# One temporary of a float64 conversion in PSUM, and two sums of block products written over their PSUM banks

## The chip, the cores and the metric

The kernel runs on one NeuronCore of a Trainium2 chip. The metric is the device time of one execution in microseconds (us), the median of several executions. The engines are named as in the profile: PE is TensorE (its weight loads stand apart as PEld), DVE is VectorE, ACT is ScalarE, POOL is GpSimd, SP is SyncE, whose queue issues nearly all DMAs.

## The reference

Three layers are computed one after the other. First a banded attention with a distance bias (2 batches, 8 heads, 768 positions, width 64). Then a mixture of experts over 1536 tokens, of which the reference is

```python
for e in range(E):                        # E = 4, D = 512, F = 1024
    h = np.maximum(x @ w1[e], 0.0)
    out += p[:, e:e + 1] * (h @ w2[e])
```

Then a last layer, whose weights `w_in`, `w_out` and `g_ln` arrive as float64:

```python
h = x @ w_in
sm = softmax(h); solu = h * sm
ln = (solu - mean) / sqrt(var + 1e-06) * g_ln
return (ln @ w_out).astype(np.float32)
```

## The kernel before, in words

There are two arms; the inputs choose the fast one (`fast_arm`), and only its instructions run. Names that begin with `f` (`fg`, `fhh`, `fhl`, `fr`, `fwS`) are its tiles.

**Precision.** Every float32 matrix is held as a high and a low part in float32r, and a product is three matmuls: high by high, high by low, low by high. A matmul has 128 rows, 128 columns of weights and 512 columns of tokens, and writes one PSUM bank (`fg`, six banks in turn).

**The mixture.** Each of the four experts is cut into two halves of the hidden width, so there are eight half experts, `he` 0 to 7; "period" below is one half expert. From `he` 1 on, one half expert is (`moe`, L490 ff.):

1. the tokens 1024 to 1535 in eight groups of 12 matmuls (`gemm_groups`): four groups "up" (`g1`, L450), each followed by a Relu on ACT that makes the high part `fhh` (L456) and a DVE instruction that makes the low part `fhl` (L457); then four groups "down" (`g2`, L469), each followed by a DVE product with the expert's weight (L479, into one of the two halves of `tmp2`) and a POOL addition to the accumulator in `scr` (L480). Down needs all four `fhl`;
2. the tokens 0 to 1023 upwards in 14 block products of 6 matmuls, 84 in all (`paired_groups`, L530), combined from sums of blocks. ACT copies three of the partial results to SBUF (`kept`, L535, in the buffer `kr`), DVE adds a kept one and a bank (L538), ACT takes the Relu (L517) and DVE makes the low part (L518);
3. the same tokens down: two times four groups of 12 matmuls (L469), each group with L479 on DVE and L480 on POOL.

So a half expert is 96 + 84 + 96 = 276 matmuls.

**Work done beside it.** After each group the function `tick` lays more work into the queues: weights of the next half expert are loaded (L265), their high part is made on ACT (L279) and their low part on POOL (L287); POOL forms sums of weight blocks (L328 to L331). Between them stands the conversion of the last layer's weights from float64 to two float32r parts, in 32 pieces of 256 numbers a partition (`from_f64`, `conv_steps`). A piece has the steps load (L354), nothing, `one` (L189 to L192), `both` (L196 to L198, and L360 for the second 16 pieces, which scales by `g_ln`), `parts` (L363, L364) and store (L367). Each counted tick does one step, and a new piece begins every third counted tick; the ticks after the second and third up group and most of those in the block products are not counted. So after nearly each down group DVE gets one of `one` (4 instructions), `both` (3 or 4) and `parts` (2). All DVE instructions stand in one queue that is worked through in order: whatever `tick` put ahead of an L479 or L457 is done first.

The conversion has two temporaries of 256 columns, `af` and `ff` (as integers `a` and `f`), both at the end of the SBUF buffer `kr` (columns 2048 to 2559). The raw piece `fr` holds 64-bit numbers, of which `high` and `low` are every second 32-bit word, and is overwritten by the two parts. Before the change all operands of all these instructions are in SBUF.

Besides the six banks of `fg`, two PSUM banks belong to the pool `ps3a`, opened before the mixture; its tile `h3` is first used by the last layer (`g3`, L664).

Of the kernel before, what the change touches and what calls it, by code (L numbers as in the profile page):

```python
# [8 lines left out]
F32 = mybir.dt.float32  # L9
# [6 lines left out]
ALU = mybir.AluOpType  # L16
# [34 lines left out]
def kernel(ctx, tc, ep, qk, vp, nn, pr, wall, w64, gl, out):  # L51
    nc = tc.nc
# [18 lines left out]
    gt = const.tile([128, 8], F32, name="gt")  # L71
# [12 lines left out]
    krf = kr.rearrange("p a b c -> p (a b c)")  # L84
# [29 lines left out]
    with tc.manual_schedule():  # L114
# [27 lines left out]
        def iota(cols, step, base, cm):  # L142
# [23 lines left out]
                                       op0=ALU.is_le, op1=ALU.mult)  # L166
        nc.vector.scalar_tensor_tensor(out=fi, in0=ng, scalar=float(NG_MAX), in1=flg[:, 1:2],
                                       op0=ALU.is_le, op1=ALU.mult)
# [5 lines left out]
        flag = nc.values_load(fi[:1, :1], min_val=0, max_val=1)  # L174


    def from_f64(raw):

        w = raw.bitcast(I32).rearrange("p (c w) -> p c w", w=2)
        low = raw.bitcast(U32).rearrange("p (c w) -> p c w", w=2)[:, :, 0]  # L180
        high = w[:, :, 1]
        af, ff = (krf[:, 2048 + 256 * j:2304 + 256 * j] for j in range(2))
        a, f = af.bitcast(I32), ff.bitcast(I32)
        halves = raw.bitcast(F32R).rearrange("p (w c) -> p w c", w=2)
        v = nc.vector

        def one():

            v.tensor_scalar(a, high, 3, 0x3FFFFFFF, op0=ALU.logical_shift_left, op1=ALU.bitwise_and)  # L189
            v.scalar_tensor_tensor(out=f, in0=high, scalar=-2 ** 30, in1=a, op0=ALU.bitwise_and, op1=ALU.bitwise_or)  # L190
            v.tensor_scalar(a, high, 0x7FFFFFFF, None, op0=ALU.bitwise_and)  # L191
            v.scalar_tensor_tensor(out=ff, in0=a, scalar=float(897 << 20), in1=ff, op0=ALU.is_ge, op1=ALU.mult)  # L192

        def two():

            v.tensor_scalar(a, f, -2 ** 23, None, op0=ALU.bitwise_and)  # L196
            v.scalar_tensor_tensor(out=af, in0=low, scalar=2.0 ** -52, in1=af, op0=ALU.mult, op1=ALU.mult)  # L197
            v.tensor_tensor(out=ff, in0=ff, in1=af, op=ALU.add)  # L198

        return one, two, ff, halves  # L200

    def stream(arm):

# [4 lines left out]
        st = St()  # L208
# [135 lines left out]
        def conv_steps():  # L344

            c = st.next_conv
            if c >= 32 or st.cvp is None:
                return None
            st.next_conv += 1
            raw = st.cvp.tile([128, 256], I64, tag="r64", name=f"{arm}r64", bufs=2)  # L350
            one, two, ff, halves = from_f64(raw)

            def load():
                nc.sync.dma_start(out=raw, in_=w64[c])  # L354

            def both():
                two()
                if c >= 16:
                    j = (c - 16) // 2
                    nc.vector.tensor_scalar(ff, ff, gt[:, j:j + 1], None, op0=ALU.mult)  # L360

            def parts():
                nc.vector.tensor_copy(out=halves[:, 0], in_=ff)  # L363
                nc.vector.tensor_tensor(out=halves[:, 1], in0=ff, in1=halves[:, 0].bitcast(F32), op=ALU.subtract)  # L364

            def store():
                nc.sync.dma_start(out=w_dram[c // 2, :, :, 256 * (c % 2):256 * (c % 2) + 256], in_=halves.bitcast(F32))  # L367
                st.stored += 1

            return [load, nothing, one, both, parts, store]  # L370
# [125 lines left out]
        def paired_groups(he, h1, h2):  # L496

            lo, hi = slice(0, HALF), slice(HALF, 2 * HALF)

            def raw_x(k0, cols):  # L500
                return [[x[:, k0 + j, cols] for j in range(2)] for x in (xh, xl)]

            right = {1: raw_x(0, lo), 2: raw_x(2, lo), 3: raw_x(2, hi), 4: raw_x(0, hi)}
            for i, f in ((5, 0), (6, 1), (7, 2)):
                right[i] = [[xt[:, f, b, j] for j in range(2)] for b in range(2)]
            banks, kept = {}, {}

            def left(q, i):
                n = 8 * he + 2 * q
                w, k0 = {1: (st.pieces[n], 0), 2: (st.pieces[n], 2), 4: (st.pieces[n + 1], 2), 6: (st.pieces["S", n], 0),  # L510
                         3: (st.pieces["S", n], 2), 7: (st.pieces["S", n + 1], 0), 5: (st.pieces["S", n + 1], 2)}[i]
                return w.rearrange("p w (k f) -> p w k f", k=4)[:, :, k0:k0 + 2]

            def hidden(src, dst, ft):
                th = st.hp.tile([128, HALF], F32R, tag="hh", name=f"{arm}hh")
                tl = st.hp.tile([128, HALF], F32R, tag="hl", name=f"{arm}hl")
                nc.scalar.activation(th, src, AF.Relu)  # L517
                nc.vector.scalar_tensor_tensor(out=tl, in0=src, scalar=0.0, in1=th.bitcast(F32),  # L518
                                               op0=ALU.max, op1=ALU.subtract)
                dst[0][ft], dst[1][ft] = th, tl  # L520

            def product(q, i):
                c = {1: "a", 6: "a", 7: "a", 4: "a", 2: "b", 5: "c", 3: "c"}[i]
                if i in (1, 2, 5):
                    banks[q, c] = st.psp.tile([128, 512], F32, tag="g", name=f"{arm}g")
                ps = banks[q, c]
                w, x = left(q, i), right[i]
                for j in range(2):
                    for m, (a, b) in enumerate(((0, 0), (0, 1), (1, 0))):
                        nc.tensor.matmul(ps, lhsT=w[:, a, j], rhs=x[b][j],  # L530
                                         start=(i in (1, 2, 5) and j == 0 and m == 0), stop=(j == 1 and m == 2),
                                         skip_group_check=(i not in (1, 2, 5)))
                if i in (1, 6, 7):
                    kept[q, i] = sc_b[(2 if i == 6 else 0) + q]
                    nc.scalar.copy(kept[q, i], ps)  # L535
                if i in (2, 7, 3):
                    t = kept[q, {2: 1, 7: 7, 3: 6}[i]]
                    nc.vector.tensor_tensor(out=t, in0=t, in1=banks[q, "b" if i == 2 else "c"], op=ALU.add)  # L538
                    hidden(t, *((h1, 2 * q) if i == 2 else (h2, 2 * q + 1) if i == 7 else (h2, 2 * q)))
                elif i == 4:  # L540
                    hidden(ps, h1, 2 * q + 1)

            for i in (1, 2, 6, 5, 7, 4, 3):
                for q in range(2):
                    product(q, i)
                yield i
            for j in range(4):
                st.free["R", j] = he + 1
            if he < NHE - 1:
                for q in (0, 2):  # L550
                    form_steps(8 * he + 8 + q, st.now)
            else:
                st.second += range(14)
# [71 lines left out]
    def rest_of_moe(st, arm, gen):  # L625
        with ExitStack() as es:
            st.hp = hp = es.enter_context(tc.tile_pool(name=f"{arm}h", bufs=8))
            st.wS = es.enter_context(tc.tile_pool(name=f"{arm}wS", bufs=1)).tile([128, 4, 2, 512], F32R, name=f"{arm}wS")
            st.cvp = es.enter_context(tc.tile_pool(name=f"{arm}cvp", bufs=2))
            st.ps3 = es.enter_context(tc.tile_pool(name=f"{arm}ps3a", bufs=1, space=PSUM))  # L630
            with tc.tile_pool(name=f"{arm}gps", bufs=6, space=PSUM) as psp:
                st.psp = psp
                for q in (0, 2):
                    st.form_steps(8 + q, st.now + 2)
                st.tick()
                for _ in gen:
                    pass
                st.drain()
            solu_layer(st, arm, hp)
# [107 lines left out]
    def fast_arm():  # L747
        st = stream("f")
        with ExitStack() as es:
# [328 lines left out]
            late.pop()()  # L1078
            tokens[0] = NT
        rest_of_moe(st, "f", gen)  # L1080


    def general_arm():
# [7 lines left out]
        with ExitStack() as es:  # L1091
# [11 lines left out]
            for i in range(NI):  # L1103
# [27 lines left out]
                for b in range(B):  # L1131
                    s = SLOTS.index((b, i))
                    for pr_ in range(4):
                        x = psX.tile([128, 128], F32, tag="x", name="gx")
                        for a in range(2):
# [34 lines left out]
                            for c in range(NI):  # L1170
# [5 lines left out]
                                                op=ALU.subtract)  # L1176
        st.x_forms()
        rest_of_moe(st, "g", moe(st, [(0, 512), (512, 512), (1024, 512)]))

    with tc.If(flag > 0) as cmp:  # L1180
# [77 lines left out]
```

## Time and profile before

| what | us |
|---|---|
| median of 3 runs (773.88 to 774.78) | 773.94 |
| the profiled execution's own time | 773.89 |
| its span in the profile | 772.0 |
| busy: PE, PEld | 746.5, 597.9 |
| busy: DVE, ACT, POOL | 565.2, 264.9, 337.7 |

Between the profiled time and the span lie 1.89 us outside the profile. A busy share is an average over stages. Of PE it overstates: matmuls are pipelined and each one's end is modelled, so that one of 128x512 is shown at 389 to 397 ns, while they start some 227 ns apart when nothing holds them up (48 in 10.89 us). The attention takes the span up to about 187 us, the mixture beside the conversion up to about 622 us, the last layer the rest.

### The profile page before, as it was taken

What the parts mean: (1) busy time and instruction counts of PE and PEld (TensorE: products, weight loads), DVE (VectorE), ACT (ScalarE), POOL (GpSimd) and SP (SyncE); (2) the same over time, 40 slices, a digit from 0 to 9 for tenths busy, and PEclk for the clock granted to TensorE, in tenths of its full rate; (3) what the DMA queues carried; (4) which work ended last, traced back from release to release, by engine and by line L of the source; (5) the groups of instructions that cost most, each with busy time, mean ns of one, the idle gap of its engine ahead of it and who ended that gap; (6) DMA issues with size and microseconds to landing.
All of it is one profiled execution on the core that took longest, in us unless ns stands there. A gap on an engine that the chain in (4) does not pass through costs nothing.

```text
span 772.0 us, 10562 instructions
## 1 busy us (share of the span) xinstructions
PE 746.5 (97%) x3710; PEld 597.9 (77%) x3710; DVE 565.2 (73%) x1052; ACT 264.9 (34%) x593; POOL 337.7 (44%) x310
## 2 busy tenths in 40 slices
PE   8889999999999999999999899989989999999997
PEld 5667766688888888888888688868868887888886
DVE  6777778522599879969979986996999646455541
ACT  5666655332313132142131213213132314233352
POOL 1000079365169439609817922970795272000001
PEclk9999999999999999999999899999998999999999
DMA  8443421112143233323423222332322650222221
GB/s 249 133 126 101 124 79 45 42 42 91 31 138 109 67 97 109 107 85 104 116 68 110 82 82 82 109 115 64 110 69 68 231 206 0 60 74 75 62 72 46
DMA packets 54015, 73.01 MB, mean 95 GB/s; under 512 B 7104, under 2 KB 31936, under 8 KB 53952
## 3 DMA queue, kind: packets, MB, share of 16 engines
q1 hardware_dynamic: 53392, 71.81, 29.9%
q8 instruction: 31, 0.51, 0.3%
q10 hardware_dynamic: 560, 0.43, 0.2%
q14 instruction: 32, 0.26, 0.1%
HBM read 56.46 MB, written 11.56 MB: 88 GB/s over the span
## 4 chain that ended last, share of the span: by engine, by line
PE 62%; DVE 21%; issue 9%; ACT 4%; POOL 3%; DMA 0%; DVEq 0%; POOLq 0%; ACTq 0%
PE fg L469 19%; PE fg L530 13%; PE fo L725 9%; PE fh L664 7%; PE fg L450 5%; DVE tmp L479 4%; PE sps L816 3%; PE x L885 3%; DVE kr L190 3%; DVE kr L197 2%; PE pt L863 2%; DVE kr L191 2%; POOL scr L480 2%; DVE fhl L518 1%; POOL xl L483 1%
## 5 line engine op out<-in xcount | busy, mean ns | idle before, releaser
L469 PE MATMUL fg<-fhh,wV 128*128 128x512 f32 (+1 forms) x800 | 255.1, 391 | 0.0
L480 POOL TENSOR_TENSOR scr<-scr,tmp 128x512 f32<-128x512 f32 x84 | 112.2, 1338 | 174.9 <-DVE tmp L479 174.9
L469 PEld LDWEIGHTS fg<-fhh,wV 128*128 128x128 f32 x800 | 152.5, 191 | 35.2 <-issue 6.3
L469 PE MATMUL fg<-fhl,wV 128*128 128x512 f32 (+1 forms) x400 | 155.7, 389 | 10.3 <-DVE fhl L457 10.0
L450 PE MATMUL fg<-xh,wR 128*128 128x512 f32 (+1 forms) x320 | 102.7, 387 | 1.4 <-DVE xl L897 1.4
L469 PEld LDWEIGHTS fg<-fhl,wV 128*128 128x128 f32 x400 | 76.5, 191 | 28.4 <-DVE fhl L457 14.1
L450 PEld LDWEIGHTS fg<-xh,wR 128*128 128x128 f32 x320 | 59.9, 188 | 17.1 <-issue 4.3
L479 DVE TENSOR_TENSOR tmp<-fg,pb 128x512 f32<-128x512 f32 x84 | 57.3, 682 | 13.2 <-PE fg L469 8.4
L450 PE MATMUL fg<-xl,wR 128*128 128x512 f32 (+1 forms) x160 | 60.6, 379 | 0.0
L841 ACT ACTIVATE p<-p,mn 128x256 f32<-128x256 f32 (+1 forms) x96 | 46.3, 484 | 41.1 <-DVE mn L835 38.6
L530 PE MATMUL fg<-xt,fwS 128*128 128x512 f32 x252 | 58.3, 389 | 0.0
L535 ACT COPY kr<-fg 128x512 f32<-128x512 f32 x42 | 23.8, 581 | 97.3 <-PE fg L530 95.7
L530 PE MATMUL fg<-xh,wR 128*128 128x512 f32 x168 | 55.1, 394 | 0.0
L530 PEld LDWEIGHTS fg<-xt,fwS 128*128 128x128 f32 x252 | 47.3, 188 | 9.8
L279 ACT CAST fwS<-kr 128x512 fp32r<-128x512 f32 x28 | 16.0, 619 | 111.0 <-POOL kr L331 111.0
L714 POOL TENSOR_SCALAR fva<-fva 128x1 f32<-128x1 f32 x12 | 3.8, 313 | 109.3 <-ACT scr L713 109.3
L518 DVE SCALAR_TENSOR_TENSOR fhl<-kr,fhh 128x512 fp32r<-128x512 f32 x42 | 29.1, 693 | 29.4 <-ACT fhh L517 29.4
L287 POOL TENSOR_TENSOR wR<-fraw,wR 128x512 fp32r<-128x512 f32 x28 | 39.9, 1433 | 18.2 <-ACT wR L279 18.2
L517 ACT ACTIVATE fhh<-kr 128x512 fp32r<-128x512 f32 x42 | 26.6, 632 | 59.3 <-DVE kr L538 59.3
L725 PE MATMUL fo<-xt,fth 128*128 128x512 f32 (+1 forms) x156 | 45.3, 375 | 0.0
L190 DVE SCALAR_TENSOR_TENSOR kr<-fr,kr 128x256 int32<-128x256 int32 x32 | 43.3, 1353 | 1.1
L538 DVE TENSOR_TENSOR kr<-kr,fg 128x512 f32<-128x512 f32 x42 | 28.6, 681 | 20.3 <-ACT kr L535 18.8
(156 smaller groups left out, 1434.2 us busy)
## 6 DMA issues: line engine op xcount, KB each, us to landing
fraw<-in_wall_dram SPq DMA_DIRECT2D x61, 256.0 KB, 2.7
fr<-in_w_dram SPq DMA_DIRECT2D x32, 256.0 KB, 2.7
w_dram<-fr SPq DMA_DIRECT2D x32, 256.0 KB, 2.4
kr<-in_wall_dram SPq DMA_DIRECT2D x28, 256.0 KB, 2.6
v<-in_vp_dram SPq DMA_DIRECT2D x10, 512.0 KB, 3.4
xt<-w_dram SPq DMA_DIRECT2D x6, 512.0 KB, 10.2
kr<-in_qk_dram SPq DMA_DIRECT2D x22, 128.0 KB, 4.0
out_dram<-scr SPq DMA_DIRECT2D x11, 256.0 KB, 2.2
```

What stands on the lines that cost most here:

```text
L190: v.scalar_tensor_tensor(out=f, in0=high, scalar=-2 ** 30, in1=a, op0=ALU.bitwise_and, op1=ALU.bitwise_or)
L287: e.tensor_tensor(out=w[:, 1], in0=t, in1=w[:, 0].bitcast(F32), op=ALU.subtract)
L450: nc.tensor.matmul(ps[:, :n], lhsT=w[:, a, k], rhs=b[:, k, cols], start=(k == 0 and i == 0), stop=(k == 3 and i == 2))
L469: nc.tensor.matmul(ps[:, :n], lhsT=w[:, a, k], rhs=b[k], start=(k == 0 and i == 0), stop=(k == 3 and i == 2))
L479: nc.vector.tensor_tensor(out=t, in0=ps[:, :n], in1=pb[:, cols], op=ALU.mult)
L480: nc.gpsimd.tensor_tensor(out=a, in0=a, in1=t, op=ALU.add)
L518: nc.vector.scalar_tensor_tensor(out=tl, in0=src, scalar=0.0, in1=th.bitcast(F32), op0=ALU.max, op1=ALU.subtract)
L530: nc.tensor.matmul(ps, lhsT=w[:, a, j], rhs=x[b][j], start=(i in (1, 2, 5) and j == 0 and m == 0), stop=(j == 1 and m == 2), skip_group_ch ...
L538: nc.vector.tensor_tensor(out=t, in0=t, in1=banks[q, "b" if i == 2 else "c"], op=ALU.add)
L664: nc.tensor.matmul(ps[:, hf], lhsT=a[:, k, cs], rhs=w[:, b], start=(k == 0 and i == 0), stop=(k == 3 and i == 2))
L725: nc.tensor.matmul(ps, lhsT=a[:, fc % 4], rhs=wo[fc][:, b, c0:c0 + n], start=(fc == 0 and i == 0), stop=(fc == 7 and i == 2))
L841: nc.scalar.activation(p[:, a, :nw], p[:, a, :nw], AF.Exp, bias=mn[:, a:a + 1], scale=-1.0, accum_out=su[:, a:a + 1])
```

## The change

Two things change; no instruction is added, removed or moved, on any engine. (On DVE the last addition of the conversion, L198, keeps its place; its output is another tile.)

- The temporary `af` moves to PSUM: the tile `cvs` of two banks with the tag `h3` of the pool `ps3a`; piece c uses the first 256 columns of bank c % 2. `ff` stays in SBUF, now at columns 2048 to 2303. The last step's result is left in `af`: by the addition itself in the first 16 pieces, by the scaling in the other 16. So every two-input instruction of the conversion has one input in SBUF and one in PSUM, and every one-input instruction either writes or reads PSUM.
- Of the three sums in the block products (products 2, 7 and 3) those of 2 and 3 are written over the PSUM bank that was one of their inputs, instead of over the kept SBUF buffer. The Relu (L517) and the low part (L518) then read PSUM. Product 7's sum stays in SBUF, since its bank goes on accumulating.

```diff
-    def from_f64(raw):
+    def from_f64(raw, af):
...
-        af, ff = (krf[:, 2048 + 256 * j:2304 + 256 * j] for j in range(2))
+        ff = krf[:, 2048:2304]
...
-        def two():
+        def two(scale):
 
             v.tensor_scalar(a, f, -2 ** 23, None, op0=ALU.bitwise_and)
             v.scalar_tensor_tensor(out=af, in0=low, scalar=2.0 ** -52, in1=af, op0=ALU.mult, op1=ALU.mult)
-            v.tensor_tensor(out=ff, in0=ff, in1=af, op=ALU.add)
+            if scale is None:
+                v.tensor_tensor(out=af, in0=ff, in1=af, op=ALU.add)
+            else:
+                v.tensor_tensor(out=ff, in0=ff, in1=af, op=ALU.add)
+                v.tensor_scalar(af, ff, scale, None, op0=ALU.mult)
+
+        def parts():
+            v.tensor_copy(out=halves[:, 0], in_=af)
+            v.tensor_tensor(out=halves[:, 1], in0=af, in1=halves[:, 0].bitcast(F32), op=ALU.subtract)
...
-            one, two, ff, halves = from_f64(raw)
+            one, two, parts, halves = from_f64(raw, st.cvs[:, c % 2, 0:256])
...
-                    t = kept[q, {2: 1, 7: 7, 3: 6}[i]]
-                    nc.vector.tensor_tensor(out=t, in0=t, in1=banks[q, "b" if i == 2 else "c"], op=ALU.add)
+                    s, u = kept[q, {2: 1, 7: 7, 3: 6}[i]], banks[q, "b" if i == 2 else "c"]
+                    t = s if i == 7 else u
+                    nc.vector.tensor_tensor(out=t, in0=s, in1=u, op=ALU.add)
...
+            st.cvs = st.ps3.tile([128, 2, 512], F32, tag="h3", name=f"{arm}cvs")
```

## Rows read from the trace of the kernel before

**Rows 1.** The page: busy time, share of the span, instructions of two engines.
```profile
PE   746.5 (97%) x3710; PEld 597.9 (77%) x3710; DVE 565.2 (73%) x1052; ACT 264.9 (34%) x593; POOL 337.7 (44%) x310
```

**Rows 2.** Waits of PE: line, releaser, us in total, times, longest us.
```profile
PE fg L469 <- DVE fhl L457: 10.0, 7, 1.7
```

**Rows 3.** Chain of waits in time, 190 to 622: start us, us, what.
```profile
248.08 10.28 PE fg L469 x44
...
311.28 10.26 PE fg L469 x44
...
374.44 10.28 PE fg L469 x44
384.72 19.21 PE fg L530 x84
403.94 10.89 PE fg L469 x48
...
441.05 12.76 PE fg L469 x44
...
510.11 10.31 PE fg L469 x44
...
576.76 13.13 PE fg L469 x44
```

**Rows 4.** Windows: stretch, its length; busy PE, PEld, DVE, ACT, POOL; clock, DMA.
```profile
406.83:437.62 30.79, 29.97 (x133) 24.48 (x131) 30.10 (x37) 7.40 (x14) 26.98 (x24) 1.00 0.32 98
441.10:447.90 6.80, 6.80 (x19) 5.39 (x20) 6.59 (x11) 0.00 (x0) 4.23 (x4) 0.61 0.47 154
509.40:516.20 6.80, 6.09 (x27) 5.01 (x28) 6.66 (x11) 0.00 (x0) 5.04 (x4) 1.00 0.48 142
```

**Rows 5.** Timeline of DVE, 403 to 443: start us, us, engine, line, instruction.
```profile
406.83 0.68 DVE L479 TENSOR_TENSOR tmp<-fg,pb 128x512 f32<-128x512 f32 x1
...
433.59 1.40 DVE L197 SCALAR_TENSOR_TENSOR kr<-fr,kr 128x256 f32<-128x256 uint32 x1
435.02 1.40 DVE L198 TENSOR_TENSOR kr<-kr 128x256 f32<-128x256 f32 x1
...
437.62 0.68 DVE L457 SCALAR_TENSOR_TENSOR fhl<-fg,fhh 128x512 fp32r<-128x512 f32 x1
...
440.32 1.87 DVE L457 SCALAR_TENSOR_TENSOR fhl<-fg,fhh 128x512 fp32r<-128x512 f32 x3
```

**Rows 6.** Timeline of POOL, same stretch.
```profile
433.37 1.34 POOL L480 TENSOR_TENSOR scr<-scr,tmp 128x512 f32<-128x512 f32 x1
434.66 1.47 POOL L287 TENSOR_TENSOR wV<-fraw,wV 128x512 fp32r<-128x512 f32 x1
```

**Rows 7.** DVE by line: count, shortest/median/longest ns, first and last start, shape.
```profile
L190 DVE SCALAR_TENSOR_TENSOR kr<-fr,kr x32: 853/1401/1420, 193.5 to 612.9; 128x256 int32<-128x256 int32 x32
L191 DVE TENSOR_SCALAR kr<-fr x32: 293/296/1278, 194.9 to 614.4; 128x256 int32<-128x256 int32 x32
L198 DVE TENSOR_TENSOR kr<-kr x32: 424/1392/1411, 198.0 to 617.9; 128x256 f32<-128x256 f32 x32
L479 DVE TENSOR_TENSOR tmp<-fg,pb x84: 676/679/693, 187.1 to 631.6; 128x512 f32<-128x512 f32 x84
```

**Rows 8.** DVE L518 by line, its first input in SBUF (kr) or in PSUM (fg).
```profile
L518 DVE SCALAR_TENSOR_TENSOR fhl<-kr,fhh x42: 691/693/695, 200.8 to 611.4; 128x512 fp32r<-128x512 f32 x42
L518 DVE SCALAR_TENSOR_TENSOR fhl<-fg,fhh x14: 681/682/684, 212.1 to 607.4; 128x512 fp32r<-128x512 f32 x14
```

**Rows 9.** Timeline of SP, same stretch: a store and the next load.
```profile
417.22 0.53 SPq L367 DMA_DIRECT2D w_dram<-fr  x1
...
419.70 0.33 SPq L354 DMA_DIRECT2D fr<-in_w_dram  x1
```

**Rows 10.** Waits of DVE line L479, by line: releaser, us in total, times.
```profile
  POOL scr L480: 4.7, 2
```

**Rows 11.** DMA issues, 403 to 443: KB each, median us to landing.
```profile
fr<-in_w_dram SPq DMA_DIRECT2D x4, 256.0 KB, 2.6
```

More of the change, by code (lines that the diff above doesn't have):

```diff
@@ L192, in one @@
             v.scalar_tensor_tensor(out=ff, in0=a, scalar=float(897 << 20), in1=ff, op0=ALU.is_ge, op1=ALU.mult)
-        def two():
+        def two(scale):
             v.tensor_scalar(a, f, -2 ** 23, None, op0=ALU.bitwise_and)
             v.scalar_tensor_tensor(out=af, in0=low, scalar=2.0 ** -52, in1=af, op0=ALU.mult, op1=ALU.mult)
-            v.tensor_tensor(out=ff, in0=ff, in1=af, op=ALU.add)
-        return one, two, ff, halves
+            if scale is None:
[6 more added lines that the diff above has]
+            v.tensor_tensor(out=halves[:, 1], in0=af, in1=halves[:, 0].bitcast(F32), op=ALU.subtract)
+        return one, two, parts, halves
     def stream(arm):
@@ L356, in both @@
             def both():
[L357 to L364, printed above, removed]
+                two(gt[:, (c - 16) // 2:(c - 16) // 2 + 1] if c >= 16 else None)
             def store():
```

## The prediction

> **What bounds the kernel now.** I read the page's busy times first: PE is busy for 97% of the span, DVE for 73% [rows 1]. PE's own waits come next: in the whole span it lost time worth naming to one partner alone, the low part `fhl` (L457, DVE), 7 times, 10.0 us [rows 2]. That sum is too small, since an issue gap counts as idle only from a matmul's modelled end, so I take the loss from the chain of waits. It gives the pace without a stall: 84 matmuls of the block products in 19.21 us, 48 of the down groups in 10.89 us [rows 3]. A half expert is 84 + 4 x 48 matmuls, hence 19.21 + 4 x 10.89 = 62.77 us. The same chain marks six points at which PE went on behind a late `fhl`: 248.08, 311.28, 374.44, 441.05, 510.11 and 576.76 us. The five distances are 63.20, 63.16, 66.61, 69.06 and 66.65 us, which is 0.43, 0.39, 3.84, 6.29 and 3.88 us over the pace, 14.83 us together.
>
> Why is `fhl` late? Take the period before 441.05. DVE's first down product starts at 406.83 and the first L457 at 437.62 [rows 5]. PE ended the up group that this L457 belongs to at about 403.94 + 9 x 2.72 = 428.4 (2.72 us = a quarter of 10.89), so DVE is 9 us behind. In those 30.79 us DVE was busy for 30.10 [rows 4]: 8 products of 0.68 us (5.4 us) and 28 instructions of the conversion, which took 30.79 - 5.4 = 25.4 us, **0.905 us each** with their gaps.
>
> Why does one take that long? The shortest L198, with two SBUF inputs, took 0.424 us, the median 1.392; L190 and L191 scatter likewise, L191 from 0.293 to 1.278 [rows 7]. Beside it on the clock: L197 starts at 433.59 and ends at 434.99, L198 at 435.02 and ends at 436.42 [rows 5]; POOL's instructions end at 434.71 and 436.13 [rows 6]. Each DVE instruction ends 0.28 us behind the POOL instruction that was running when it began: it was held until POOL let go. L479 has the same kind of operation on twice the columns, but one input in PSUM, and all 84 took 0.676 to 0.693 us [rows 7], POOL running or not. So the wait belongs to instructions whose operands are all in SBUF.
>
> **The change, part by part.**
>
> *Conversion.* No instruction is added, so the sum is 28 instructions of a new length. After the change none has all operands in SBUF. For two inputs, one of them in PSUM, I halve L479's columns: by L198's shortest (0.424 for 256 columns) and SBUF against PSUM at 512 (0.693 against 0.682, [rows 8]) it is 0.41 to 0.42. For one input, out of or into PSUM: 0.42 too. It loses the fast form of 0.29 [rows 7], which I take to be lost with PSUM. No row shows DVE writing PSUM. Bounds: 0.29 below (today's fast form), 1.42 above (L190's longest, held by POOL) [rows 7]; I take 0.42, nearest to L198's shortest and L479. With a gap of 0.03 (434.99 to 435.02) 28 of them make 12.6 us, with the products 18.0, in place of 30.8. From the first product to the end of the first up group DVE has 428.4 - 406.8 = 21.6 us, so L457 starts when ACT has its Relu. Within one group's 2.72 us the longest lot is four instructions and a product, 4 x 0.45 + 0.68 = 2.5 us: nothing piles up.
>
> The point from which it decides: PE ends the fourth up group at 403.94 + 12 x 2.72 = 436.6 and needs the first `fhl` there, so L457 (0.68) may start at 435.9 at the latest; (435.9 - 406.83 - 5.4) / 28 = **0.84 us** an instruction. Twice my estimate still hides it.
>
> [...]
>
> *What goes.* The stalls, and with them a loss of clock. [...] So the terms are:
> - the five distances above: 14.83 us, of which 12.76 - 10.31 = 2.45 is clock;
> - the stall that ends at 248.08, alike in place to the next two: 0.43 us;
> - the slow stretch behind 576.76: 13.13 - 10.28 = 2.85 us.
>
> Together **18.1 us**, 12.8 of stalls and 5.3 of clock.
>
> *Covers.* A faster DVE asks earlier for the raw pieces. Today a store goes out at 417.22 and the load into its buffer at 419.70 [rows 9], landing 2.6 us later [rows 11]. Afterwards `parts` of the first piece follows the third product: PE's group ends at 403.94 + 3 x 2.72 = 412.1, plus 0.68 + 2 x 0.45 gives 413.7; store and load end at 413.7 + 2.5 + 2.6 = 418.8. The piece is wanted behind the seventh product, at 423.0 + 0.68 = 423.7. Cover: 4.9 us; without it DVE, and all in its queue, would wait for the rest.
>
> *Two sums over their banks.* 28 of the 42 low parts read PSUM: 0.011 us less each, 0.3 us of DVE in all [rows 8], in stretches where PE waits for nothing (the 84 matmuls hold their pace). The banks are held longer, until a Relu and a low part (0.69 us, [rows 8]) have read them; the next groups on them come after others, and need those same low parts anyway. I put it at zero; if a bank were wanted at once, it would cost some two times 0.69 us a half expert.
>
> *The rest.* Attention and last layer keep their instructions. Sum: 773.89 (the profiled execution, 0.05 below the median) - 18.1 = **755.8 us**.
>
> **The rivals.**
>
> *POOL becomes the late one.* It was busy 26.98 of the 30.79 us [rows 4], and L479 has already waited for its additions twice, 4.7 us [rows 10], since `tmp2` has two halves only. Against it: POOL's time there seems to include waits for DVE that go too (1.47 us beside 1.34 for the same size, [rows 6]), and L457 has 435.9 - 428.4 = 7.5 us, less one Relu, to spare. If it leaves half of the three long stalls (1.9 us each) and one slow stretch (2.6), it is 755.8 + 5.7 + 2.6 = 764.1.
>
> *The clock falls all the same.* Two slow stretches, not tied to stalls: 755.8 + 5.3 = 761.1. For: behind one of three equal stalls it did not fall, so stalls alone don't set it. Against: behind the three short stalls the 44 matmuls kept their 10.26 to 10.28 us [rows 3].
>
> *PE's lateness only changes hands*, or the SBUF operand that remains is held by POOL as before: no change, 773.9.
>
> *Slower.* The wait for POOL stays in the conversion whatever the operands, and the one-input instructions lose their fast form: of the 28, 14 (L189, L191, L196, L360, L363) go from 0.29 to 0.42, 1.8 us; in the first three periods, without L360, 11, 1.4 us. DVE is already over the point of 0.84, so all of it turns into stall: 3 x 1.8 + 3 x 1.4 = 9.6, **783.5 us**. [...] Against the mechanism stand the 84 L479, none above 0.693 us, though they read SBUF and write it beside POOL.
>
> **How the numbers follow.** Forecast 0.77 (with the spread of the single terms 754.3 to 757.5), POOL 0.08, clock 0.07, no change 0.04, slower 0.04. The range from 754.0 to 761.5 takes in the forecast and the clock, and leaves out 0.16. Faster by over 0.2% (1.5 us, about what a measurement of this kernel can tell from no change): 0.92; within it 0.04; slower 0.04.
>
> **What would show it.** Right: the conversion's lines all near 0.42 us and none near 1.4, DVE's busy time down by more than 100 us (304 instructions at 0.45 us less would be 138, too much since the early pieces wait less), no wait of PE for L457, six periods of about 62.8 us, granted clock 1.00 in all of them. POOL's additions should shorten too. Wrong: instructions that write PSUM at 0.84 us or more; PE's wait for L457 still there with L479 waiting for POOL; a clock of 0.6 without a stall before it; the time made up again behind 622 us.

## The result, and the profile after

The changed kernel took **755.51 us** (median of 4 runs, 755.48 to 755.99) against 773.91 us beside it (772.49 to 774.78): a ratio of 0.9765, 95% interval 0.9749 to 0.9782. Forecast were 755.8 us and a range of 754.0 to 761.5. The profiled execution took 755.48 us with a span of 753.7, 18.3 below the span before.

The page: busy time of the engines, then the shares of the chain that ended last, by engine.

```profile
PE 738.7 (98%) x3710; PEld 594.7 (79%) x3710; DVE 447.2 (59%) x1052; ACT 265.0 (35%) x593; POOL 321.5 (43%) x310
...
PE 93%; ACT 2%; DVE 2%; DMA 0%; POOL 0%; issue 0%; ACTq 0%
```

DVE lost 118 us of busy time [rows 1] and POOL 16, though neither has an instruction less; the chain now runs through PE almost alone (PE had 62% of it before and DVE 21%). (The lines of code have moved: L450 is now L451, L456 L457, L457 L458, L469 L470, L479 L480, L480 L481, L482 L483, L483 L484, L517 L518, L518 L519, L530 L531, L535 L536, L538 L540, and L363 and L364 are L205 and L206.)

The waits of PE, longest first; the last of these lines is the only one that the mixture beside the conversion has left, the first two lie in the attention.

```profile
PE wp L135 <- DVE eps L137: 1.4, 1, 1.4
PE fg L451 <- DVE xl L900: 1.4, 1, 1.4
...
PE fg L531 <- ACT kr L536: 1.0, 1, 1.0
```

The line of [rows 2], the wait for the low part, is gone. The chain of waits in order of time (start us, us, what) answers to [rows 3]:

```profile
246.92 10.88 PE fg L470 x48
...
309.65 10.88 PE fg L470 x48
...
372.38 10.88 PE fg L470 x48
383.25 19.23 PE fg L531 x84
402.48 21.76 PE fg L470 x96
424.24 10.88 PE fg L451 x48
435.12 10.88 PE fg L470 x48
...
497.85 10.88 PE fg L470 x48
...
560.58 10.88 PE fg L470 x48
571.46 2.73 PE fg L531 x12
```

Every half expert now takes 62.73 us, five times running, at PE's pace without a stall. From 185 to 640 us the chain has 44 pieces; before it had 518, many of them through DVE.

The DVE instructions by line (count, shortest/median/longest ns), to be held against [rows 7]; `fcvs` is the temporary in PSUM:

```profile
L189 DVE TENSOR_SCALAR fcvs<-fr x32: 415/417/419, 193.1 to 595.4; 128x256 int32<-128x256 int32 x32
L190 DVE SCALAR_TENSOR_TENSOR kr<-fr,fcvs x32: 420/420/422, 193.5 to 595.9; 128x256 int32<-128x256 int32 x32
L191 DVE TENSOR_SCALAR fcvs<-fr x32: 427/427/428, 194.0 to 596.3; 128x256 int32<-128x256 int32 x32
L192 DVE SCALAR_TENSOR_TENSOR kr<-fcvs,kr x32: 423/424/424, 194.4 to 596.8; 128x256 f32<-128x256 int32 x32
L202 DVE TENSOR_SCALAR fcvs<-kr,gt x16: 486/489/491, 410.0 to 599.5; 128x256 f32<-128x256 f32 x16
L205 DVE CAST fr<-fcvs x32: 411/414/416, 203.2 to 600.9; 128x256 fp32r<-128x256 f32 x32
L206 DVE TENSOR_TENSOR fr<-fcvs,fr x32: 423/424/425, 203.6 to 601.3; 128x256 fp32r<-128x256 f32 x32
```

Where a line had spread from 0.3 or 0.4 to 1.4 us, no two executions of it now differ by more than 5 ns. POOL's additions (L481) keep their median, 1.293 us against 1.296 before, but the long ones are gone: the longest takes 1.327 us, where it had taken 1.484, and the mean falls from 1.338 to 1.294. DVE's waits in the mixture name no load of a raw piece, so the cover that the prediction worked out held.

The same stretch as in [rows 4] and [rows 5], from the first down product to the first low part, in the windows (columns as in [rows 4]) and in DVE's timeline:

```profile
405.40:427.60 22.20, 22.20 (x100) 18.39 (x99) 16.73 (x36) 5.20 (x10) 19.63 (x19) 1.00 0.32 102
```

```profile
405.31 0.69 DVE L480 TENSOR_TENSOR tmp<-fg,pb 128x512 f32<-128x512 f32 x1
...
425.18 0.69 DVE L480 TENSOR_TENSOR tmp<-fg,pb 128x512 f32<-128x512 f32 x1 [1.15 <-POOL scr L481]
...
427.69 0.69 DVE L458 SCALAR_TENSOR_TENSOR fhl<-fg,fhh 128x512 fp32r<-128x512 f32 x1
428.30 0.41 DVE L205 CAST fr<-fcvs 128x256 fp32r<-128x256 f32 x1
428.75 0.42 DVE L206 TENSOR_TENSOR fr<-fcvs,fr 128x256 fp32r<-128x256 f32 x1
430.41 0.69 DVE L458 SCALAR_TENSOR_TENSOR fhl<-fg,fhh 128x512 fp32r<-128x512 f32 x1 [1.24 <-ACT fhh L457]
```

From first product to first low part it is 22.4 us now, it was 30.8; and DVE is idle for a quarter of the window. From the second low part on DVE waits for ACT's Relu, that is, for PE.

One wait is new. Here are POOL's and ACT's timelines of the last half expert, where POOL also makes the low part `xl` of the finished accumulator (L484) from the high part that ACT copies (L483):

```profile
574.17 1.29 POOL L484 TENSOR_TENSOR xl<-scr,xh 128x512 fp32r<-128x512 f32 x1 [0.73 <-PE fg L531]
575.42 1.29 POOL L481 TENSOR_TENSOR scr<-scr,tmp 128x512 f32<-128x512 f32 x1
```

```profile
576.75 0.62 ACT L483 CAST xh<-scr 128x512 fp32r<-128x512 f32 x1 [2.65 <-POOL scr L481]
577.27 1.07 ACT L536 COPY kr<-fg 128x512 f32<-128x512 f32 x2
```

PE needs ACT's copy of a block product (L536) at about 576.7 us. It stands in ACT's queue behind the copy of `xh`, that one waits for POOL's fourth addition, and that one stands in POOL's queue behind a low part that waited for ACT's previous copy (573.48 to 574.10; this row puts the wait down to PE, those of the other three groups to ACT's `xh`). One group of this exchange takes 3.27 us (573.48 to 576.75 for L483), a down group on PE 2.72. The next matmul starts 1.40 us behind the last instead of 0.23, by the starts in the trace, and the one after it 0.34: a loss of 1.17 + 0.11 us.

### The profile page after: what moved, and what is told of

Read it like the earlier page. It is cut to its first block, busy times and chain, and to the rows that moved or that the text cites. A ratio compares the mean times of both kernels' runs of the same rounds, so it can differ in the third digit from the quotient of the medians.

```text
span 753.7 us, 10598 instructions
## 1 busy us (share of the span) xinstructions
PE 738.7 (98%) x3710; PEld 594.7 (79%) x3710; DVE 447.2 (59%) x1052; ACT 265.0 (35%) x593; POOL 321.5 (43%) x310
## 4 chain that ended last, share of the span: by engine, by line
PE 93%; ACT 2%; DVE 2%; DMA 0%; POOL 0%; issue 0%; ACTq 0%
PE fg L470 35%; PE fg L531 18%; PE fg L451 14%; PE fo L728 9%; PE fh L667 9%; PE sps L819 3%; PE x L888 3%; PE pt L866 2%; ACT p L844 1%; DVE p L838 1%; ACT pts L868 0%; PE fpt L708 0%; DVE xl L900 0%; PE wp L959 0%; PE g L907 0%; DMA kr<-in_qk_dram 0%
## 5 line engine op out<-in xcount | busy, mean ns | idle before, releaser
L470 PE MATMUL fg<-fhh,wV 128*128 128x512 f32 (+1 forms) x800 | 251.3, 385 | 0.0
L481 POOL TENSOR_TENSOR scr<-scr,tmp 128x512 f32<-128x512 f32 x84 | 108.4, 1294 | 165.0 <-DVE tmp L480 165.0
L470 PEld LDWEIGHTS fg<-fhh,wV 128*128 128x128 f32 x800 | 149.9, 188 | 34.5 <-issue 6.3
L470 PE MATMUL fg<-fhl,wV 128*128 128x512 f32 (+1 forms) x400 | 152.4, 381 | 0.0
L451 PE MATMUL fg<-xh,wR 128*128 128x512 f32 (+1 forms) x320 | 102.7, 387 | 1.4 <-DVE xl L900 1.4
L480 DVE TENSOR_TENSOR tmp<-fg,pb 128x512 f32<-128x512 f32 x84 | 57.9, 690 | 58.6 <-PE fg L470 51.0
L470 PEld LDWEIGHTS fg<-fhl,wV 128*128 128x128 f32 x400 | 75.2, 188 | 13.8
L451 PEld LDWEIGHTS fg<-xh,wR 128*128 128x128 f32 x320 | 59.9, 188 | 17.1 <-issue 4.3
L458 DVE SCALAR_TENSOR_TENSOR fhl<-fg,fhh 128x512 fp32r<-128x512 f32 (+1 forms) x40 | 26.6, 664 | 57.8 <-ACT fhh L457 57.7
L451 PE MATMUL fg<-xl,wR 128*128 128x512 f32 (+1 forms) x160 | 60.6, 379 | 0.0
L531 PE MATMUL fg<-xt,fwS 128*128 128x512 f32 x252 | 58.4, 390 | 1.0 <-ACT kr L536 1.0
L536 ACT COPY kr<-fg 128x512 f32<-128x512 f32 x42 | 24.3, 584 | 93.9 <-PE fg L531 93.9
L531 PEld LDWEIGHTS fg<-xt,fwS 128*128 128x128 f32 x252 | 47.2, 188 | 11.2 <-ACT kr L536 1.4
L531 PE MATMUL fg<-xh,wR 128*128 128x512 f32 x168 | 55.1, 394 | 0.0
L457 ACT ACTIVATE fhh<-fg 128x512 fp32r<-128x512 f32 (+1 forms) x40 | 22.9, 573 | 66.7 <-PE fg L451 66.7
L295 POOL TENSOR_TENSOR wR<-fraw,wR 128x512 fp32r<-128x512 f32 x28 | 36.0, 1296 | 18.2 <-ACT wR L287 18.2
L295 POOL TENSOR_TENSOR wV<-fraw,wV 128x512 fp32r<-128x512 f32 x28 | 36.0, 1296 | 15.7 <-ACT wV L287 15.7
L519 DVE SCALAR_TENSOR_TENSOR fhl<-fg,fhh 128x512 fp32r<-128x512 f32 x42 | 28.3, 688 | 18.6 <-ACT fhh L518 18.6
```

The source lines that it names most:

```text
L295: e.tensor_tensor(out=w[:, 1], in0=t, in1=w[:, 0].bitcast(F32), op=ALU.subtract)
L451: nc.tensor.matmul(ps[:, :n], lhsT=w[:, a, k], rhs=b[:, k, cols], start=(k == 0 and i == 0), stop=(k == 3 and i == 2))
L458: nc.vector.scalar_tensor_tensor(out=tl, in0=ps[:, :n], scalar=0.0, in1=th.bitcast(F32), op0=ALU.max, op1=ALU.subtract)
L470: nc.tensor.matmul(ps[:, :n], lhsT=w[:, a, k], rhs=b[k], start=(k == 0 and i == 0), stop=(k == 3 and i == 2))
L480: nc.vector.tensor_tensor(out=t, in0=ps[:, :n], in1=pb[:, cols], op=ALU.mult)
L481: nc.gpsimd.tensor_tensor(out=a, in0=a, in1=t, op=ALU.add)
```

## The experiments

All times are medians beside runs of the kernel before on the same chip; ratios are to those, with 95% intervals.

**The conversion alone.** The sums go back over the kept buffers:

```diff
-                    s, u = kept[q, {2: 1, 7: 7, 3: 6}[i]], banks[q, "b" if i == 2 else "c"]
-                    t = s if i == 7 else u
-                    nc.vector.tensor_tensor(out=t, in0=s, in1=u, op=ALU.add)
+                    t = kept[q, {2: 1, 7: 7, 3: 6}[i]]
+                    nc.vector.tensor_tensor(out=t, in0=t, in1=banks[q, "b" if i == 2 else "c"], op=ALU.add)
```

> The conversion's temporary in PSUM, the three sums back over the kept SBUF buffers. Theory (DVE was held in the conversion by POOL, and only there did PE wait): 755.5 us within 0.7, all conversion lines at 0.41 to 0.49 us as in the changed kernel. Rival (the sums carry part of the gain, by freeing the kept buffers or by quicker Relus): above 757 us.

Measured: 755.75 us, ratio 0.9769 (0.9754 to 0.9784). The whole gain lies in the conversion.

**The sums alone.** The reverse edit, on the kernel before.

> The sums over their banks, the conversion as before with both temporaries in SBUF. Theory: no difference from the kernel before, 773.9 us within 1.5 (0.3 us of DVE in all, in stretches where PE waits for nothing); conversion lines still with medians near 1.4 us, PE's wait for L457 still there. Rival (the sums carry part of the gain): below 772 us.

Measured: 773.51 us, ratio 0.9998 (0.9989 to 1.0008): nothing. PE's wait for the low part is there, almost as before (10.0 us, 7 times, in [rows 2]):

```profile
PE fg L469 <- DVE fhl L457: 9.6, 6, 1.7
```

**Instruction by instruction.** The temporary stays in PSUM, but the result is left in the SBUF temporary, so that the last three instructions have all operands in SBUF:

```diff
-            if scale is None:
-                v.tensor_tensor(out=af, in0=ff, in1=af, op=ALU.add)
-            else:
-                v.tensor_tensor(out=ff, in0=ff, in1=af, op=ALU.add)
-                v.tensor_scalar(af, ff, scale, None, op0=ALU.mult)
+            v.tensor_tensor(out=ff, in0=ff, in1=af, op=ALU.add)
+            if scale is not None:
+                v.tensor_scalar(ff, ff, scale, None, op0=ALU.mult)
...
-            v.tensor_copy(out=halves[:, 0], in_=af)
-            v.tensor_tensor(out=halves[:, 1], in0=af, in1=halves[:, 0].bitcast(F32), op=ALU.subtract)
+            v.tensor_copy(out=halves[:, 0], in_=ff)
+            v.tensor_tensor(out=halves[:, 1], in0=ff, in1=halves[:, 0].bitcast(F32), op=ALU.subtract)
```

> The changed kernel, but the conversion's result stays in the SBUF temporary as before: the scaling and the two instructions that make the parts have all operands in SBUF again, the others one in PSUM. Theory (it is the operands that decide, instruction by instruction): within one execution the lines with a PSUM operand stay at 0.41 to 0.43 us with hardly any spread, while the subtraction of the parts has a median of 1.3 us or more, and scaling and cast go between 0.28 and 1.3 us. PE stays covered: (21 x 0.45 + 7 x 0.85 + 5.4 = 20.8 us, below the 29.1 that hide), 755.5 us within 1. Rival (the conversion as a whole got out of POOL's step): those lines fall too, all below 0.6 us.

Measured: 756.27 us (two runs), ratio 0.9769 (0.9743 to 0.9796). Four of its lines, the first with one PSUM input, the others without (L200 is the scaling, L203 and L204 the parts):

```profile
L198 DVE TENSOR_TENSOR kr<-kr,fcvs x32: 420/420/423, 196.6 to 599.2; 128x256 f32<-128x256 f32 x32
L200 DVE TENSOR_SCALAR kr<-kr,gt x16: 353/687/1483, 409.9 to 599.7; 128x256 f32<-128x256 f32 x16
L203 DVE CAST fr<-kr x32: 275/316/1390, 203.1 to 601.0; 128x256 fp32r<-128x256 f32 x32
L204 DVE TENSOR_TENSOR fr<-kr,fr x32: 424/1396/1421, 203.4 to 601.3; 128x256 fp32r<-128x256 f32 x32
```

In one execution, side by side with POOL's same work, the line with a PSUM operand has no spread, and the all-SBUF ones go from their own time to 1.0 to 1.1 us more. The rival, that the conversion merely fell out of step with POOL, is out: L204 is as slow as it was. PE is covered all the same; these instructions are 7 of the 28.

**POOL's part.** On the kernel before, POOL's additions are left out (the sum over the half experts is missing from the result; the products are still made):

```diff
-                    nc.gpsimd.tensor_tensor(out=a, in0=a, in1=t, op=ALU.add)
```

> The kernel before, without POOL's additions to the accumulator (the sum over the half experts is left out; DVE still forms every product). Theory (POOL's instructions hold DVE's): in the period before 441.05 the 28 instructions took 25.4 us, of which about 10.6 are their own (half at 0.31, half at 0.45, with gaps), so 14.8 us of holding over 24 POOL instructions; with 8 of the 24 gone some 9.9 remain, 20.5 + 5.4 = 25.9 us, below 29.1: stalls and the loss of clock go, 756 us, up to 760. Medians of the conversion's lines fall. Rival (the long instructions have another cause, as the stride of the 64-bit words or waits on the instruction before): conversion lines as before, 773.9 us.

Measured: 754.06 us, ratio 0.9745 (0.9722 to 0.9768). With all of the conversion still in SBUF, the lines of [rows 7] read

```profile
L190 DVE SCALAR_TENSOR_TENSOR kr<-fr,kr x32: 424/1133/1408, 193.5 to 595.2; 128x256 int32<-128x256 int32 x32
L191 DVE TENSOR_SCALAR kr<-fr x32: 293/1264/1281, 193.9 to 596.6; 128x256 int32<-128x256 int32 x32
L198 DVE TENSOR_TENSOR kr<-kr x32: 424/426/1399, 196.7 to 602.1; 128x256 f32<-128x256 f32 x32
```

L198's median falls from 1.392 to 0.426 us and L190's from 1.401 to 1.133, while L191's rises: who is held moves with where POOL's remaining instructions fall. The traces show it execution by execution. In the kernel before, the 14 L198 beside which no POOL instruction runs take 0.424 to 0.428 us and the 18 others 1.391 to 1.411; here 18 take 0.424 to 0.427 and 14 take 0.845 to 1.399. L190, which reads every second word, takes 0.424 to 0.429 here in the 13 cases without POOL. So POOL holds them, not the stride of the 64-bit words and not the instruction ahead. The time is 1.4 us below the changed kernel's; the trace has no wait of PE for ACT's copy at the place where that one has its new wait.

**How much DVE can bear.** On the changed kernel, a copy from PSUM to PSUM behind every instruction of the conversion (its result is not read); a second run does so behind every second one (`every` is 1 or 2):

```diff
+        class V:
+            def __getattr__(self, name):
+                def call(*args, **kw):
+                    getattr(nc.vector, name)(*args, **kw)
+                    count[0] += 1
+                    if count[0] % every == 0:
+                        nc.vector.tensor_copy(out=more, in_=af)
+                return call
...
+            more = st.cvs[:, c % 2, 256:512]
```

> The changed kernel, with one more copy PSUM to PSUM (256 columns of the temporary into unused columns of its bank) behind every instruction of the conversion; nothing of it is read. Theory (what PE waits for is DVE's backlog alone, deciding point 0.84 us an instruction of the original kind): two instructions of 0.45 with gap make 0.90, over the point. In the late three periods 56 x 0.45 + 5.4 = 30.6 us against the 29.1 that hide, so stalls of about 1.5 and 1.8 us each, 10 us in all; the early three (50 x 0.45 + 5.4 = 27.9) stay hidden. 755.5 + 10 = 765.5 us, up to 771 if the clock falls behind two of the stalls. POOL's additions stay at 1.29 us, none held. Rival (PE's stalls came from POOL being held by DVE, not from DVE's queue): 755.5 us, since these copies touch no SBUF.

Measured: 764.73 us, ratio 0.9893 (0.9874 to 0.9911). The sum was met and its place was not. In the period of [rows 5], by DVE's timeline, the first low part starts 28.2 us behind the first product (L495 is the product here, L473 the low part, L546 the block products, L551 ACT's copy):

```profile
405.53 0.68 DVE L495 TENSOR_TENSOR tmp<-fg,pb 128x512 f32<-128x512 f32 x1
...
433.71 0.68 DVE L473 SCALAR_TENSOR_TENSOR fhl<-fg,fhh 128x512 fp32r<-128x512 f32 x1
...
435.77 1.88 DVE L473 SCALAR_TENSOR_TENSOR fhl<-fg,fhh 128x512 fp32r<-128x512 f32 x3
```

The 56 instructions took 28.2 - 5.4 = 22.8 us, 0.81 a pair and not the 0.90 expected, for a copy often starts 0.34 us behind its instruction. That is just under the deciding point of 0.84, and the first low part indeed came in time: it is ready at 434.39 us, and PE takes it at 435.39. What PE waited for was the second one. It stands behind four more instructions of the conversion and its copies, starts at 435.77 us, and PE, which could have taken it at 436.07, did so at 436.51:

```profile
436.51 0.50 PE L485 MATMUL fg<-fhl,wV 128*128 128x512 f32 x1 [0.28 <-DVE fhl L473]
```

With the 0.34 us to the next start instead of 0.23 this cost 0.55 us in each late period. The rest came later: most of it in the block products, where DVE was still behind and ACT's copies with it, and some 1.2 us at the last layer's first wait:

```profile
PE fg L546 <- ACT kr L551: 4.9, 3, 2.5
```

POOL's additions kept 1.293 us and the clock did not fall. So DVE's backlog alone, with no POOL instruction held, makes PE wait.

> The changed kernel with a further copy PSUM to PSUM behind every second instruction of the conversion. Theory (deciding point 0.84 us an original instruction; the copies came to some 0.81 with the instruction they follow where every one had a copy): 42 x 0.41 + 5.4 = 22.6 us against 29.1, all hidden, 755.5 us within 1. Rival (every instruction more on DVE costs time, half of what every one having a copy cost): 760 us.

Measured: 755.99 us, ratio 0.9765 (0.9744 to 0.9785): 144 more instructions for nothing, as a cover should have it. Of these two numbers of copies, only the one that brings DVE to about 0.8 us an instruction costs time.

**Why the late periods were worse.** On the kernel before, the scaling by `g_ln` is left out (the factor is missing from the result):

```diff
-                if c >= 16:
-                    j = (c - 16) // 2
-                    nc.vector.tensor_scalar(ff, ff, gt[:, j:j + 1], None, op0=ALU.mult)
```

> The kernel before, without the scaling by g_ln in the second 16 pieces (the factor is left out of the result): 25 in place of 28 instructions in the late periods. Theory (the long stalls of the late three periods are these three instructions over the deciding point, and the loss of clock came with the long stalls): late periods become like the early ones, 63.2 us, 3 x 3.4 = 10.2 us of stall and 5.3 us of clock less, 758.5 us; granted clock 1.00 throughout. Rival (the clock falls on its own): 763.8 us with stretches at a clock of 0.6.

Measured: 763.72 us, ratio 0.9861 (0.9838 to 0.9883). Half right. The periods did become alike: the chain's marks lie at 375.98, 439.17 and 502.32 us, 63.2 apart, and no slow stretch follows them: the 44 matmuls behind each take 10.25 to 10.30 us, and from 190 to 585 us the granted clock is 1.00. But 5 us turned up elsewhere. The chain of the last half expert leaves PE for 23 us (in this run L447 is the up groups, L477 POOL's addition, L479 ACT's copy `xh`, L532 its copy of a block product, L527 the block products):

```profile
559.95 1.83 PE fg L447 x8
561.78 0.02 issue
561.80 1.47 POOL wV L287
...
582.32 1.31 POOL scr L477
583.64 0.02 issue
583.66 0.02 ACT xh L479
...
584.19 0.58 ACT kr L532
584.77 0.04 issue
584.82 7.37 PE fg L527 x24
```

It is the wait that the changed kernel has at 576.7 us, here 3.7 us long, and behind it the clock was at its lower level (0.50 of full speed) for 3.4 us: the 24 matmuls of the last row took 7.37 us, where the pace makes 5.5. So the time is the rival's, but not by the rival's way. In the kernel before, PE, late by the earlier stalls, came to this place at 595.2 us and went on without a wait.

**That wait.** POOL makes the low part of a group behind the next group's addition:

```diff
-                        nc.gpsimd.tensor_tensor(out=xl[:, dt, cols], in0=a, in1=xh[:, dt, cols].bitcast(F32),
-                                                op=ALU.subtract)
+                        for low in st.low:
+                            low()
+                        st.low = [lambda a=a: nc.gpsimd.tensor_tensor(
+                            out=xl[:, dt, cols], in0=a, in1=xh[:, dt, cols].bitcast(F32), op=ALU.subtract)]
+                        if dt == 3:
+                            st.low.pop()()
```

> The changed kernel; in the last half expert POOL makes the low part xl of a down group behind the addition of the next group, not before it. Theory (the one new wait of PE, 1.2 us at 576.5 us, is ACT's copy of a block product standing in ACT's queue behind the copy xh that waits for POOL's fourth addition, and POOL and ACT hand work back and forth once for every group): that wait goes, 1.2 to 1.4 us less, 754.2 us. Rival (POOL has simply too much work in that stretch): no change, 755.5 us.

Measured: 754.68 us, ratio 0.9757 (0.9744 to 0.9771). The wait is gone from the trace and the span is 752.6 us, 1.1 below. As 0.8 us between runs that did not stand side by side says little, both were run again on one chip:

> The changed kernel itself, on the same chip as the next run, to compare the two: 755.5 us within 0.5.

> The changed kernel with the low part xl of the last half expert one group later on POOL. Theory (the wait of 1.17 + 0.11 us for ACT's copy was POOL and ACT handing work back and forth): 1.1 to 1.3 us below the run of the changed kernel beside it. Rival (the wait comes back elsewhere): no difference.

Measured: the changed kernel 756.09 us (755.48 to 757.44), this one 754.58 (754.20 to 754.89), five runs each. The changed kernel is 0.1 us above what was expected of it. The two don't overlap, so this version is quicker than both kernels, by 1.5 us here. On the kernel without scaling the same edit did little:

> The kernel before without the scaling (the factor is left out of the result), and the low part xl of the last half expert one group later on POOL. [...] Rival (POOL is simply behind there, held by DVE's conversion): 763.7 us.

Measured: 762.05 us, ratio 0.9837 (0.9817 to 0.9857), 1.7 below the run without it, and the wait is still 3.1 us long (3.34 between starts). The 759 to 760.5 us that were expected did not come; the time lies between them and the rival's 763.7. The wait that is left is the rival's: with the conversion in SBUF, DVE's products and with them POOL's additions come too late, also with POOL's low parts behind. POOL's fourth addition waits for DVE's product here:

```profile
580.61 1.26 POOL L478 TENSOR_TENSOR scr<-scr,tmp 128x512 f32<-128x512 f32 x1 [1.29 <-DVE tmp L477]
```

## Why the prediction was right

**What bounds.** DVE's late low part, its six places and their price: right. The sixth mark, 576.76 us, is the fifth matmul of a down group; in the changed kernel that one starts at 561.32. That is 15.44 us earlier, of which 0.12 lies ahead of the mixture; the terms up to there said 14.83 + 0.43 = 15.26.

**The cause.** Right, and now shown from three sides: operand by operand in one execution, by taking away a part of POOL's work, and by giving DVE its backlog back without POOL. With one SBUF input the subtraction L206 takes 0.424 us, with two (L204 of the run with the result in SBUF) it has a median of 1.396. The one-input lines were held too while all their operands were in SBUF (L191 up to 1.278 us, [rows 7]), and are not with one in PSUM (L191 now 0.427 to 0.428). What DVE and POOL share there, no run here shows.

**The price of an instruction.** 0.42 us taken, 0.414 to 0.429 measured, and 0.489 for the scaling, which was put too low. Nothing in the trace before showed DVE writing PSUM; it costs what reading it does (L189 writes it in 0.417 us, L205 reads it in 0.414). The 0.682 against 0.693 us of [rows 8] is a fair comparison, since no POOL instruction runs beside any of these L518; it says nothing of being held. L192, with one input in PSUM, has a median of 0.424 us, and L198 had 0.424 at its shortest with both in SBUF [rows 7]: no difference. The fast form was lost, as taken (L189's median was 0.284 us before, 0.417 now; L191's shortest 0.293, now 0.427).

**The deciding point.** 0.84 us an instruction was worked out for the first low part, and at 0.81 that one was in time. The prediction passed over the second: PE wants it three matmuls (0.68 us) later, and DVE has two more instructions (`parts`) to do before it. By the rows of the run with a copy behind every instruction its point is (436.07 - 0.69 - 405.53 - 5.4 - 0.6) / 30 = 0.80 us (0.69 for the low part itself, 0.6 for the first one), and with 0.81 it cost 0.55 us a period. In the three early periods of the kernel before, too, it is this one alone that PE waited for (the mark 248.08 is the fifth matmul of its group). With 0.42 us an instruction either point is far off, so the forecast did not suffer. The 42 instructions in place of 28 cost nothing.

**Clock.** 5.3 us forecast, and no slow stretch in the mixture of the changed kernel, where the granted clock is 1.00 from 190 to 606 us. In the kernel before it fell at 439.5 and 576.1 us, within the second of two stalls of about 2 us, and stood at 0.50 of full speed for 6.8 us each time (0.61 over the second stretch of [rows 4], which ends after it). In two other runs it fell behind one stall of 3.7 or 3.1 us (behind them 24 matmuls took 7.37 us and 31 took 8.95, where the pace makes 5.5 and 7.1). It did not fall each time: the double stall that ended at 510.11 us had no fall [rows 4]. That the stalls cause it is likely by this and was not tried by itself. The 5.3 us were read off the two slow stretches of one trace.

**The two sums.** No time forecast, none found.

**What the sum missed.** Two items, nearly equal. The new wait, 1.17 + 0.11 us, is the rival "POOL becomes the late one" in small, at another place than was named: not `tmp2` (L480 did wait for POOL 6 times, 6.9 us, at no cost to PE), but ACT's queue. Against it the last layer's first wait, at 641.4 us before, became 0.96 us shorter (1.42 us between starts, now 0.46): ACT's exponential stands behind the last copy of `xh`, and that behind POOL's additions. In the last half expert's final groups DVE's conversion had delayed these: from the first to the third they took 7.66 us (612.77 to 620.43, where POOL waited 0.83 us for DVE's product), now 6.54 (595.58 to 602.12). The remaining 0.5 us lies in small steps of 0.1 to 0.2 us: ahead of the mixture, in the stalls and their slow stretches, and at the end. That the forecast hit to 0.3 us is in part luck, since the two items offset each other.

## What to carry to other kernels

Here an engine that works through its queue in order was held by another and looked merely busy (DVE, 30.10 of 30.79 us, [rows 4]). The signs were a wide spread between a line's shortest and median time (0.424 and 1.392 us), and ends that follow the other engine's ends (by a median of 0.28 us). Splitting a line's executions by what runs beside them shows it at once. Moving one operand of each instruction elsewhere was enough, even though some of the new forms are slower on their own (0.417 against 0.28 us). What decided was whether the queue then kept ahead of the engine that bounds (at 0.81 us an instruction, against a deciding point of 0.80, it did not): a point that one can work out, for each thing that the engine waits for, and test with idle instructions. When stalls go, look for what they had covered: here a POOL–ACT exchange that had cost nothing while PE was late.

## What the runs showed of the hardware that had not been expected

- The scaling by a factor for each partition, from SBUF to PSUM, takes 0.486 to 0.491 us for 256 columns, some 0.07 more than the other one-input forms with PSUM (0.411 to 0.428).
- In the run with a copy behind every instruction, a DVE copy from PSUM to PSUM (256 columns) took 0.43 us and often started 0.34 us behind its predecessor, ahead of that one's shown end.
- The granted clock also fell without the mixture's stalls. In two profiled executions it was at its lower level (0.50) for 3.4 us in the attention at about 46 us (0.91 over the 20 us around it), and in two others at about 152 us (0.83 over the 10 us around it in one of them), each time behind a wait of PE of 0.9 to 1.4 us. The same waits stand in the other traces without a fall. These four executions took 0.7 to 1.4 us more than the median of their kernel.
